# The next batch's z evacuated whole and spread by DMA, VectorE empties one score bank in ten, some VectorE work moved, and the fixed order starts at step ten

## The chip, the cores and the metric

The kernel runs on one core of one Trainium2 chip. The metric is the device time of one execution in microseconds. Before the change the median of three runs is 2632.43 us.

## The reference, cut to what matters

An attention without softmax over 8 batches is followed by a mixture of experts over its rows:

```
scores = (z @ z.T) / S                 # per batch: z is 2496 x 64, S = 2496
out    = relu(scores) ** 2 @ v         # v is 2496 x 256
x      = (u * out).reshape(19968, 256)
logits = x @ w_gate                    # 8 experts
# the (token, expert) pairs in falling order of logit; a token goes to the first expert with room (2496 each)
y[tokens of e] = relu(x[tokens of e] @ w1[e]) @ w2[e]
```

Everything is float32. The kernel splits each operand of a matmul in two parts, hi and lo, and adds three products (hi by hi, lo by hi, hi by lo).

## The kernel before

**Steps.** The attention is a chain of 800 steps, n = 100 b + 20 g + kt: b is the batch, g one of five groups of 512 queries (the last has 448), kt one of 20 tiles of 128 keys (the last has 64 rows). In step n TensorE (PE) adds a key tile to the two accumulators of its group, six matmuls (L893 to L896). What they read, `hi` and `lo`, is made four steps earlier from `r`: ScalarE (ACT) squares `r` in place (L864), ACT (L869) or VectorE (DVE, L871) rounds it to `hi`, DVE subtracts to get `lo` (L880). In this text "step 46" and the like are counted within a batch.

**Tens.** `r` comes from scores made ten at a time. At each step whose number ends in 0 PE writes the scores of steps n+4 to n+13, in five pairs (three matmul pairs each, L851), into PSUM banks named `sc`, of which there are six. Each bank is emptied by one rectification, relu and scale, on ACT (L860). The stretch from the first score matmul of one ten to that of the next is called "ten 0" to "ten 90" below, after its first step; the ten of steps 50 to 59 is ten 50. Whatever else takes an `sc` bank (the transposes of z and of finished outputs) takes it between two tens, in a rotation.

**Around them.** At the end of a group DVE and ACT copy the accumulators out (`at`, L902 and L904), PE transposes them (L916), DVE multiplies by u (L927) and then makes 32 partial dot products with the gate's weights (`lt`, L944, "logits"), one per expert and 128 tokens. A `settle` (L73 to L91) finds the best expert of each of a batch's tokens; it stands at step 46 of the next batch.

**The z of the next batch** is prepared during a batch, for five groups g: loaded with SP's queue (`zin`, L773 and L776, 128 rows by 4 tiles), transposed on PE into an `sc` bank (`z_turn`, L807, at steps 41, 45, 49, 53 and 57), and a step later emptied by `z_parts`: per half of the partitions an ACT copy to `zh` (L818) and a DVE subtraction to `zl` (L819). The score matmuls use two halves of 64 partitions at a time, so every tile must stand in both halves. After the last group `swap_z` copies the missing halves by four DMAs (L824, L825).

**Order.** On PE, ACT and DVE the instructions stand in the order in which the code writes them (`manual_schedule`), from step -4 on. The SP queue is filled by a scheduler. A lookup `todo` tells what stands at which step.

Of the kernel before, what the change touches and what calls it, by code (L numbers as in the profile page):

```python
# [705 lines left out]
def attention(tc, u, v, z, w_gate, xd, identf, made, first, scale):  # L706
# [16 lines left out]
    with ExitStack() as ctx:  # L723
# [44 lines left out]
            return src[b, :NT * 128].rearrange("(p i) d -> p i d", i=NT)  # L768

        def load(src, b, g, name, width, copies):  # L770
            t = io.tile([128, 4, width], F32, name=name)
            n = min(4, NT - 4 * g)
            nc.sync.dma_start(t[:, :n], rows(src, b)[:, 4 * g:4 * g + n])  # L773
            if n < 4:
                for c in range(copies):
                    nc.sync.dma_start(t[c * TL:(c + 1) * TL, n], src[b, NT * 128:])  # L776
            return t
# [16 lines left out]
        def z_turn(b, g):  # L794
            if g == 0:
                ZH[b] = zp.tile([128, KT * 128], F32R, name="zh")
                ZL[b] = zp.tile([128, KT * 128], F32R, name="zl")
            p = ps.tile([128, 512], F32, name="sc", bufs=SCB)
            c = slice(512 * g, 512 * g + 512)
            t = ZI.pop((b, g))  # L800
            if (b, g) == (0, 0):
                for i in range(4):
                    nc.tensor.transpose(p[:, i * 128:i * 128 + 128], t[:, i].rearrange("p s d -> p (s d)"), identf)
                return (nc.scalar.activation(ZH[b][:, c], p, AF.Copy),
                        nc.vector.tensor_sub(ZL[b][:, c], p, ZH[b][:, c].bitcast(F32)))
            for i in range(2):
                nc.tensor.transpose(p[:, i * 128:i * 128 + 128],  # L807
                                    t[:, 2 * i:2 * i + 2].rearrange("p s d -> p (s d)"), identf)
            ZT[b, g] = p

        def z_parts(b, g):
            c = slice(512 * g, 512 * g + 512)
# [28 lines left out]
        def scores(lo, hi):  # L841
            for n in range(lo, hi, 2):
# [9 lines left out]
                                         start=key is ZH and query is ZH, stop=key is ZL)  # L852
                for s in range(2):
                    SC[n + s] = pair[s]
                    rectify(n + s)

        def rectify(n):
            p = SC.pop(n)
            r = wk.tile([128, 512], F32, name="r", bufs=GO + 3)[:, :p.shape[1]]
            recent["r"] = nc.scalar.activation(r, p, AF.Relu, scale=scale)  # L860
            R[n] = r

        def square(n):
# [1 line left out]

        def split_hi(n):
            h = wk.tile([128, 512], F32R, name="hi", bufs=LA + 1)[:, :width(seq[n][1])]
            if n % 5 < 3:
                nc.scalar.activation(h, R[n], AF.Copy)  # L869
            else:  # L870
                nc.vector.tensor_copy(h, R[n])  # L871
            HI[n] = h
# [110 lines left out]

        def logits_at(m0):
            if m0 + KT < B * NQ * KT:
                return [m0 + GO] * 14 + [m0 + KT] * 14 + [m0 + KT + 4 + i for i in range(4)]
            return [m0 + GO] * 16 + [m0 + GO + 1 + i // 3 for i in range(16)]

        for c in range(0, (B - 1) * NT // 16 * 16, 16):
            at((B * NQ - 1) * KT + 2 + c // 16, premask, c, c + 16)  # L990
        for b in range(B - 1):
            at(((b + 1) * NQ + 2) * KT + 6, settle, b * NT, (b + 1) * NT)
        at(B * NQ * KT, settle, (B - 1) * NT, (B - 1) * NT + 4 * (NQ - 1))
        at(B * NQ * KT, premask, (B - 1) * NT // 16 * 16, JP - 16)
        for b in range(B):
# [17 lines left out]
                at(B * NQ * KT + 3, settle, B * NT, J)  # L1013
            if b:
                for g in range(NQ):
                    m = n0 - 3 * KT + 4 * g + 1
                    at(m - 5, load_z, b, g)
                    at(m, z_turn, b, g)
                    at(m + 1, z_parts, b, g)
                    at(n0 - KT + 4 * g - 8, load_v, b, g)  # L1020
                at(n0 - 3 * KT + 4 * NQ + 2, swap_z, b, slice(0, KT * 128))
                for kt in range(KT):
                    at(n0 - KT + kt, split_v, b, kt)
            else:
# [27 lines left out]
        for n in range(-LA, N + 4 * E):  # L1052
            if n == 2:
                early.close()
            if n == -LA:
                fixed.enter_context(tc.manual_schedule(
                    engines={mybir.EngineType.PE, mybir.EngineType.Activation, mybir.EngineType.DVE}))
            if n == N - 4:
# [42 lines left out]
```

## Time and profile before

| what | value |
|---|---|
| median of three runs (lowest, highest) | 2632.43 us (2632.39, 2635.14) |
| the profiled execution | 2634.49 us |
| its span in the trace | 2632.2 us |
| last attention matmul starts | 1505.7 us |
| PE, DVE, ACT, POOL busy | 97%, 77%, 59%, 14% of the span |

The profiled execution lies 2.06 us above the median, and its span 2.3 us below its own time. Engine shares are averages over the attention and the experts' part, which begins when the attention ends. PE is almost always busy, so time can only come from gaps on PE, from matmuls that stand still within their "busy" time, or from matmuls at a lower clock.

### The profile page before, as it was taken

The page shows a single profiled execution, that of the slowest core. Times are in us where ns is not written, and L with a number is a line of the kernel's source. Part 1 is how long each engine was busy: PE and PEld are TensorE (multiplying, and loading weights), DVE is VectorE, ACT ScalarE, POOL GpSimd, SP SyncE. Part 2 cuts the span into 40 slices and gives each one's busy share as a digit, 9 for nine tenths or more (in the row PEclk, how much of TensorE's full clock was granted, in tenths as well). Part 3 has the DMA queues.
Part 4 walks back from the last instruction along what each step waited for, and adds up shares of the span by engine and source line. Part 5 has one row for each costly group of instructions (what it writes and reads, how often), then busy time and mean ns, then how long its engine had stood idle before and what let it go on. Part 6 is the DMA issues. An engine that isn't in the chain of part 4 may idle for free.

```text
span 2632.2 us, 44683 instructions
## 1 busy us (share of the span) xinstructions
PE 2550.8 (97%) x16328; PEld 2142.8 (81%) x16328; DVE 2027.4 (77%) x6142; ACT 1545.2 (59%) x2934; POOL 366.5 (14%) x507
## 2 busy tenths in 40 slices
PE   7999999999999999999999989999999999999998
PEld 5778787787787787787877768888898989889997
DVE  5788788898898898898888878878686868686322
ACT  7788788787788787887888512333333333333332
POOL 2000000000000000000000002242333333334331
PEclk9999999999999999999999989999999999999999
DMA  4121121210220121121200011112121212121110
GB/s 138 41 71 56 40 67 44 58 62 32 63 72 26 53 72 39 41 72 37 68 32 19 22 41 40 55 56 65 44 69 45 70 44 68 45 85 59 45 43 24
DMA packets 71644, 139.61 MB, mean 53 GB/s; under 512 B 12160, under 2 KB 39680, under 8 KB 71424
## 3 DMA queue, kind: packets, MB, share of 16 engines
q1 hardware_dynamic: 56320, 95.84, 11.6%
q0 software_dynamic: 15104, 40.91, 4.9%
q8 instruction: 128, 2.10, 0.3%
q14 instruction: 92, 0.75, 0.1%
HBM read 85.60 MB, written 40.89 MB: 48 GB/s over the span
## 4 chain that ended last, share of the span: by engine, by line
PE 76%; DVE 13%; ACT 6%; issue 3%; DMA 1%; POOL 0%; POOLq 0%; DVEq 0%; ACTq 0%; SPq 0%
PE acc L893 11%; PE acc L896 11%; PE acc L895 10%; PE sc L851 10%; PE y L602 5%; PE hp L571 5%; PE y L604 5%; PE y L603 5%; PE hp L572 5%; PE hp L573 5%; ACT r L864 2%; DVE lt L944 2%; PE srch L243 2%; DVE lo L880 2%; PE xp L555 1%
## 5 line engine op out<-in xcount | busy, mean ns | idle before, releaser
L893 PE MATMUL acc<-hi,vh 128*128 128x512 f32 (+1 forms) x1600 | 633.1, 396 | 1.7 <-DVE hi L877 1.3
L880 DVE TENSOR_TENSOR lo<-r,hi 128x512 fp32r<-128x512 f32 (+1 forms) x760 | 513.0, 678 | 149.7 <-ACT hi L869 137.2
L896 PE MATMUL acc<-hi,vl 128*128 128x512 f32 (+1 forms) x1600 | 617.9, 386 | 0.0
L895 PE MATMUL acc<-lo,vh 128*128 128x512 f32 (+1 forms) x1520 | 588.2, 387 | 0.5 <-DVE lo L880 0.2
L590 ACT ACTIVATE hh<-hp 128x512 fp32r<-128x512 f32 (+1 forms) x320 | 187.8, 587 | 548.2 <-PE hp L573 478.4
L864 ACT ACTIVATE r<-r 128x512 f32<-128x512 f32 (+1 forms) x800 | 477.0, 625 | 0.8
L944 DVE SCALAR_TENSOR_TENSOR lt<-xs,wgb 128x256 bf16<-128x256 f32 x1248 | 448.8, 421 | 0.7
L860 ACT ACTIVATE r<-sc 128x512 f32<-128x512 f32 (+1 forms) x800 | 393.0, 624 | 92.7 <-PE sc L851 91.8
L893 PEld LDWEIGHTS acc<-hi,vh 128*128 128x128 f32 x1600 | 301.5, 189 | 84.8 <-issue 30.1
L602 PE MATMUL y<-w2h,hh 128*128 128x256 f32 (+1 forms) x1280 | 366.2, 286 | 1.4 <-ACT y L629 1.4
L603 PE MATMUL y<-w2l,hh 128*128 128x256 f32 (+1 forms) x1280 | 362.4, 283 | 0.0
L869 ACT ACTIVATE hi<-r 128x512 fp32r<-128x512 f32 (+1 forms) x480 | 298.5, 622 | 106.4 <-issue 54.8
L896 PEld LDWEIGHTS acc<-hi,vl 128*128 128x128 f32 x1600 | 301.3, 188 | 56.8
L895 PEld LDWEIGHTS acc<-lo,vh 128*128 128x128 f32 x1520 | 286.9, 189 | 52.7 <-DVE lo L880 4.0
L571 PE MATMUL hp<-xh,w1h 128*128 128x512 f32 (+2 forms) x646 | 262.3, 407 | 0.7 <-ACT xh L564 0.7
L851 PE MATMUL sc<-zh 64*128 64x512 f32 (+1 forms) x800 | 224.2, 438 | 34.7 <-ACT r L860 18.5
L572 PE MATMUL hp<-xl,w1h 128*128 128x512 f32 (+2 forms) x646 | 250.7, 389 | 0.0
L602 PEld LDWEIGHTS y<-w2h,hh 128*128 128x128 f32 (+1 forms) x1280 | 240.6, 188 | 12.0 <-ACT y L629 1.8
L573 PE MATMUL hp<-xh,w1l 128*128 128x512 f32 (+2 forms) x646 | 249.5, 387 | 0.0
L603 PEld LDWEIGHTS y<-w2l,hh 128*128 128x128 f32 (+1 forms) x1280 | 240.6, 188 | 8.9
L635 POOL DMA_INDIRECT out_dram<-y,idx x160 | 184.5, 1153 | 386.7 <-ACT y L629 338.8
L496 POOL DMA_INDIRECT xg<-xd,idx x160 | 162.8, 1018 | 378.5 <-PE xp L555 133.0
(1156 smaller groups left out, 3805.7 us busy)
## 6 DMA issues: line engine op xcount, KB each, us to landing
vr<-in_v_dram SPq DMA_DIRECT2D x32, 512.0 KB, 3.7
ur<-in_u_dram SPq DMA_DIRECT2D x32, 512.0 KB, 4.3
xd<-xs SPq DMA_DIRECT2D x32, 512.0 KB, 2.9
wr<-in_moe_w_dram SPq DMA_DIRECT2D x32, 512.0 KB, 5.6
zh<-zh SPq DMA_DIRECT2D x14, 320.0 KB, 3.7
zl<-zl SPq DMA_DIRECT2D x14, 320.0 KB, 5.4
zin<-in_z_dram SPq DMA_DIRECT2D x31, 128.0 KB, 2.0
vr<-in_v_dram SPq DMA_DIRECT2D x8, 384.0 KB, 3.3
```

What stands on the lines that cost most here:

```text
L571: nc.tensor.matmul(p[:, c], wh, xh, start=(d == 0), stop=False)
L572: nc.tensor.matmul(p[:, c], wh, xl, start=False, stop=False)
L602: nc.tensor.matmul(o, h[:, c], wh, start=first, stop=False, skip_group_check=True)
L603: nc.tensor.matmul(o, h[:, c], wl, start=False, stop=False, skip_group_check=True)
L851: nc.tensor.matmul(pair[s], key[b][r, k:k + 128], query[b][r, q], start=key is ZH and query is ZH, stop=key is ZL)
L860: recent["r"] = nc.scalar.activation(r, p, AF.Relu, scale=scale)
L864: nc.scalar.activation(R[n], R[n], AF.Square)
L880: recent["l"] = nc.vector.tensor_sub(l, a, h.bitcast(F32))
L893: nc.tensor.matmul(o, vh, h, start=(kt == 0), stop=False)
L895: nc.tensor.matmul(o, vh, l, start=False, stop=False)
L896: nc.tensor.matmul(o, vl, h, start=False, stop=last)
L944: nc.vector.scalar_tensor_tensor(t[r], XS[b, g][r, i], 1.0, WG["rows"][r, e], op0=OP.mult, op1=OP.mult, accum_out=lg[r, j, e:e + 1])
```

## The change

Five edits. (1) `z_parts` and `swap_z` of batches 1 to 7 give way to `z_whole`: ACT and DVE empty the bank at full height into staging tiles `zsh` and `zsl`, of which there is one each, and eight DMAs of 64 KB per group spread them into both halves of `zh` and `zl`. The transposes stand at steps 41, 45, 51, 54 and 57, the load buffers of `zin` are two and not three. (2) In every full ten the second tile's bank is emptied by DVE (L873 after) and not by ACT; in exchange ACT rounds seven `hi` of ten and not six. (3) The logits of the third group of a batch are made 18 in the first ten and 14 in the next (before 14, 14 and 4 over the steps after), those of the fourth group 10, 14 and 8. (4) `settle` stands at step 32 and not 46. (5) The fixed order begins at step 10: before that a scheduler orders PE, ACT and DVE.

```diff
-            t = io.tile([128, 4, width], F32, name=name)
+            t = io.tile([128, 4, width], F32, name=name, bufs=2 if width == DQ else 3)
...
+        def z_whole(b, g):
+            p = ZT.pop((b, g))[:, :256]
+            h, l = [io.tile([128, 256], F32R, name=name, bufs=1) for name in ("zsh", "zsl")]
+            nc.scalar.activation(h, p, AF.Copy)
+            nc.vector.tensor_sub(l, p, h.bitcast(F32))
+            for t, src in ((ZH, h), (ZL, l)):
+                v4 = t[b][:, 512 * g:512 * g + 512].bitcast(F32).rearrange("p (i s q) -> p i s q", s=2, q=128)
+                v3 = src.bitcast(F32).rearrange("p (i q) -> p i q", q=128)
+                for s in range(2):
+                    for half in range(2):
+                        nc.sync.dma_start(v4[DQ * half:DQ * half + DQ, :, s], v3[DQ * s:DQ * s + DQ])
...
-                    rectify(n + s)
+                    rectify(n + s, n + s == lo + 1 and hi - lo == GO)
...
-            recent["r"] = nc.scalar.activation(r, p, AF.Relu, scale=scale)
+            if aside:
+                nc.vector.tensor_scalar(r, p, 0.0, scale, op0=OP.max, op1=OP.mult)
+            else:
+                recent["r"] = nc.scalar.activation(r, p, AF.Relu, scale=scale)
...
-            if n % 5 < 3:
+            if (n - LA) % GO not in (0, 4, 8):
                 nc.scalar.activation(h, R[n], AF.Copy)
...
-                return [m0 + GO] * 14 + [m0 + KT] * 14 + [m0 + KT + 4 + i for i in range(4)]
+                mid, end = {NQ - 3: (18, 14), NQ - 2: (10, 14)}.get(m0 // KT % NQ - 1, (14, 14))
+                return [m0 + GO] * mid + [m0 + KT] * end + [m0 + KT + 4 + i for i in range(4 * E - mid - end)]
...
-            at(((b + 1) * NQ + 2) * KT + 6, settle, b * NT, (b + 1) * NT)
+            at(((b + 1) * NQ + 1) * KT + 12, settle, b * NT, (b + 1) * NT)
...
-                    m = n0 - 3 * KT + 4 * g + 1
+                    m = n0 - 3 * KT + (4 * g + 1 if 4 * g + 2 < GO else KT - 3 * (NQ - g))
                     at(m - 5, load_z, b, g)
                     at(m, z_turn, b, g)
-                    at(m + 1, z_parts, b, g)
+                    at(m + 1, z_whole, b, g)
...
-                at(n0 - 3 * KT + 4 * NQ + 2, swap_z, b, slice(0, KT * 128))
...
-            if n == -LA:
+            if n == GO:
                 fixed.enter_context(tc.manual_schedule(
```

The first place is VectorE at steps 46 to 50 of a batch, before: the end of `settle`, the two halves of a `zl` behind it, and the logits of the next ten.

```order
L78 TENSOR_TENSOR code<-eq 128x19
L79 TENSOR_TENSOR oh<-code,code8b 128x152
L85 TENSOR_SCALAR sign<-m 128x19
L86 SCALAR_TENSOR_TENSOR key<-m,sign 128x19
L106 COPY rep<-key 128x152
L90 TENSOR_SCALAR top<-key 128x19
L91 CAST low<-key 128x19
L819 TENSOR_TENSOR zl<-sc,zh 64x2x128 x2
L944 SCALAR_TENSOR_TENSOR lt,lg<-xs,wgb 128x256
L880 TENSOR_TENSOR lo<-r,hi 128x512 x2
L871 CAST hi<-r 128x512
L880 TENSOR_TENSOR lo<-r,hi 128x512
```

After the change the same engine has no `settle` there. These are its rows from the last but one z of a batch (g = 3, the first `zsl` shown) to the start of ten 60; an `lo` stands between the last `zsl` and the copy of the accumulator, and then comes the rectification.

```order
L886 CAST hi<-r 128x512
L895 TENSOR_TENSOR lo<-r,hi 128x512
L892 TENSOR_TENSOR hi<-r,hi 64x512
L815 TENSOR_TENSOR zsl<-sc,zsh 128x256
L895 TENSOR_TENSOR lo<-r,hi 128x512 x2
L886 CAST hi<-r 128x512
L895 TENSOR_TENSOR lo<-r,hi 128x512
L815 TENSOR_TENSOR zsl<-sc,zsh 128x256
L895 TENSOR_TENSOR lo<-r,hi 128x512
L917 COPY at_6192<-acc_5778 128x512
L873 TENSOR_SCALAR r<-sc 128x512
L959 SCALAR_TENSOR_TENSOR lt,lg<-xs,wgb 128x256 x14
```

What moved: the score bank of each ten's second tile now waits for VectorE, and at the start of ten 60 VectorE comes to it only behind the last two `zsl`.

The second place is SP's queue over the z of a batch. Before, all loads stand ahead of the four copies:

```order
L773 DMA zin<-in_z_dram 128x256
L931 DMA xd<-xs 128x1024
L773 DMA zin<-in_z_dram 128x192
L776 DMA zin<-in_z_dram 64x64 x2
L773 DMA ur<-in_u_dram 128x768
L776 DMA ur<-in_u_dram 64x256 x2
L773 DMA zin<-in_z_dram 128x256 x3
L825 DMA zh<-zh 64x10x128
L824 DMA zh<-zh 64x10x128
L824 DMA zl<-zl 64x10x128
L825 DMA zl<-zl 64x10x128
```

After, from the second group's spread on (the last group, g = 4, is loaded in three pieces: 128x192 and twice 64x64):

```order
L821 DMA zl<-zsl 64x2x128 x4
L773 DMA zin<-in_z_dram 128x256
L776 DMA ur<-in_u_dram 64x256 x2
L773 DMA zin<-in_z_dram 128x192
L776 DMA zin<-in_z_dram 64x64
L821 DMA zh<-zsh 64x2x128 x4
L821 DMA zl<-zsl 64x2x128 x4
L776 DMA zin<-in_z_dram 64x64
L821 DMA zh<-zsh 64x2x128 x4
L821 DMA zl<-zsl 64x2x128 x4
L773 DMA zin<-in_z_dram 128x256
L821 DMA zh<-zsh 64x2x128 x4
```

What moved: forty small copies stand among the loads, and the last piece of the fifth group's load stands behind the eight copies of the third group.

The third place is PE's start. Before, behind the first transposes, come the second four score tiles in pairs and then the first accumulations:

```order
L807 MATMUL sc<-identf,zin 128x128 x2
L851 MATMUL sc<-zh 128x512 x2
L851 MATMUL sc<-zl,zh 128x512 x2
L851 MATMUL sc<-zh,zl 128x512 x2
L851 MATMUL sc<-zh 128x512 x2
L851 MATMUL sc<-zl,zh 128x512 x2
L851 MATMUL sc<-zh,zl 128x512 x2
L893 MATMUL acc_234<-hi,vh 128x512
```

After, three steps of accumulation stand there first, and the scores that follow are partly single:

```order
L807 MATMUL sc<-identf,zin 128x128 x2
L908 MATMUL acc_232<-hi,vh 128x512
L908 MATMUL acc_233<-hi,vh 128x512
...
L863 MATMUL sc<-zh 128x512
L863 MATMUL sc<-zl,zh 128x512
L911 MATMUL acc_232<-hi,vl 128x512
L911 MATMUL acc_233<-hi,vl 128x512
L908 MATMUL acc_232<-hi,vh 128x512
L910 MATMUL acc_232<-lo,vh 128x512
L863 MATMUL sc<-zh,zl 128x512
L863 MATMUL sc<-zh 128x512
```

What moved: scores now stand between accumulations, some of them without the partner that used the other 64 rows.

## Rows read from the trace of the kernel before

**Rows 1.** The page's first part: engine, busy us, share, instructions.

```profile
PE 2550.8 (97%) x16328; PEld 2142.8 (81%) x16328; DVE 2027.4 (77%) x6142; ACT 1545.2 (59%) x2934; POOL 366.5 (14%) x507
```

**Rows 2.** Windows: stretch, us, busy (count) by engine, PEclk, DMA, GB/s; batch 3.

```profile
617.20:635.94 18.74, 18.74 (x99) 15.00 (x98) 16.71 (x55) 14.24 (x27) 0.00 (x0) 1.00 0.17 56
635.94:653.33 17.39, 17.39 (x89) 13.77 (x89) 12.84 (x42) 14.33 (x27) 0.00 (x0) 1.00 0.01 1
653.33:672.80 19.47, 19.47 (x106) 15.65 (x105) 16.58 (x58) 12.56 (x25) 0.00 (x0) 1.00 0.23 67
672.80:695.94 23.14, 20.12 (x94) 15.07 (x94) 17.47 (x56) 18.59 (x36) 0.00 (x0) 0.93 0.07 19
...
750.66:766.58 15.92, 15.92 (x89) 13.73 (x88) 15.75 (x55) 14.81 (x33) 0.00 (x0) 1.00 0.30 76
```

**Rows 3.** PE's timeline at ten 30 and before ten 70: start, us, instruction.

```profile
638.13 0.44 PE L851 MATMUL sc<-zh 64*128 64x512 f32 x2
...
638.82 0.74 PE L851 MATMUL sc<-zh 64*128 64x512 f32 x2
...
639.96 0.50 PE L893 MATMUL acc<-hi,vh 128*128 128x512 f32 x1
...
716.02 0.39 PE L896 MATMUL acc<-hi,vl 128*128 128x512 f32 x1
716.34 0.50 PE L851 MATMUL sc<-zh 64*128 64x512 f32 x2
```

**Rows 4.** Timelines of ACT and of DVE at the start of ten 20.

```profile
618.20 5.01 ACT L860 ACTIVATE r<-sc 128x512 f32<-128x512 f32 x10 [0.75 <-PE sc L851]
...
624.25 0.63 ACT L869 ACTIVATE hi<-r 128x512 fp32r<-128x512 f32 x1
...
625.44 0.63 ACT L869 ACTIVATE hi<-r 128x512 fp32r<-128x512 f32 x1
...
617.54 0.68 DVE L902 COPY at<-acc 128x512 f32<-128x512 f32 x1
```

**Rows 5.** Timelines of PE, ACT and DVE around the start of ten 50.

```profile
677.94 0.49 PE L851 MATMUL sc<-zh 64*128 64x512 f32 x1 [2.62 <-ACT r L860]
...
673.87 0.38 ACT L818 ACTIVATE zh<-sc 64x256 fp32r<-64x256 f32 x1 [5.78 <-DVE zl L819]
...
670.73 0.31 DVE L73 TENSOR_REDUCE m<-lg 128x19 f32<-128x152 f32 x1
...
673.43 0.41 DVE L819 TENSOR_TENSOR zl<-sc,zh 64x256 fp32r<-64x256 f32 x1
```

**Rows 6.** Windows, sums: ten 50, ten 60 (batches 1-6), both in batch 0, ten 0 (seven).

```profile
sum 139.58, PE 121.70 PEld 91.70 DVE 106.12 ACT 111.67 POOL 0.00; mean PE 20.28 PEld 15.28 DVE 17.69 ACT 18.61 POOL 0.00
...
sum 121.75, PE 118.69 PEld 90.33 DVE 111.79 ACT 94.72 POOL 0.00; mean PE 19.78 PEld 15.06 DVE 18.63 ACT 15.79 POOL 0.00
...
sum 40.85, PE 38.61 PEld 29.18 DVE 34.47 ACT 32.66 POOL 0.00; mean PE 19.31 PEld 14.59 DVE 17.23 ACT 16.33 POOL 0.00
...
sum 136.74, PE 136.12 PEld 104.71 DVE 131.83 ACT 110.42 POOL 0.00; mean PE 19.45 PEld 14.96 DVE 18.83 ACT 15.77 POOL 0.00
```

**Rows 7.** SP's timeline, copies between halves: issue time, us.

```profile
44.95 0.59 SPq L824 DMA_DIRECT2D zh<-zh  x1
45.63 0.59 SPq L824 DMA_DIRECT2D zl<-zl  x1
...
698.86 1.07 SPq L825 DMA_DIRECT2D zl<-zl  x1
```

**Rows 8.** DMA issues (tensors, count, KB, median to landing); `zl`'s landings, first 60 us.

```profile
zh<-zh SPq DMA_DIRECT2D x8, 64.0 KB, 2.1
...
zin<-in_z_dram SPq DMA_DIRECT2D x16, 16.0 KB, 2.4
...
DMA to landing us min/median/max: 2.0/2.2/4.9
```

**Rows 9.** Waits of ACT in the first 50 us: in total, times, longest.

```profile
ACT r L860 <- PE sc L851: 5.5, 6, 2.0
```

More of the change, by code (lines that the diff above doesn't have):

```diff
@@ L854, in scores, with rectify @@
                     SC[n + s] = pair[s]
-                    rectify(n + s)
-        def rectify(n):
+                    rectify(n + s, n + s == lo + 1 and hi - lo == GO)
+        def rectify(n, aside):
             p = SC.pop(n)
             r = wk.tile([128, 512], F32, name="r", bufs=GO + 3)[:, :p.shape[1]]
-            recent["r"] = nc.scalar.activation(r, p, AF.Relu, scale=scale)
+            if aside:
+                nc.vector.tensor_scalar(r, p, 0.0, scale, op0=OP.max, op1=OP.mult)
+            else:
+                recent["r"] = nc.scalar.activation(r, p, AF.Relu, scale=scale)
             R[n] = r
```

## The prediction

> **What bounds the kernel now.** I read the page's engine shares first. PE is busy 97% of the span [rows 1], so a gain has to come out of the 3% or out of matmuls that stand still while they count as busy. The change touches the attention alone, and there one ten is like another, so the windows by tens come next. A plain ten is one without z work: ten 20 lasts 18.74 us, ten 30 lasts 17.39 [rows 2] (in ten 20 PE also transposes an output). The tens with z are longer: over batches 1 to 6 ten 50 lasts 139.58/6 = 23.26 us, ten 60 121.75/6 = 20.29 [rows 6], and ten 40 19.47 [rows 2]. Against plain ones (17.39 and 18.74) that is 5.9 + 1.55 + 0.7 us a batch.
>
> Where ten 50 loses it is seen in the three timelines at its start: `settle` takes DVE from 670.73 to 673.43; the `zl` behind it starts at 673.43; ACT's second `zh` copy waits 5.78 us for that `zl` and starts at 673.87; the rectifications queued behind it come late, and PE waits 2.62 us for a score bank until 677.94 [rows 5]. The granted clock of that ten is 0.93 [rows 2]: after this wait some matmuls ran at the lower of the two levels (1.2 against 2.4 GHz), which with the 2.62 and 2 x 0.24 for two transposes makes up the 5.9, so that it costs some 2.7.
>
> A second loss is in every ten, inside busy time. Pairs 4 and 5 of the scores start at 638.13 and 638.82, 0.69 us apart: three matmuls at 0.23. Pair 5 takes until 639.96, 1.14 us. A change from accumulation to scores costs about 0.09 (716.02 to 716.34 is 0.32 and not 0.23); I take the same for the way back. So pair 5 stands 1.14 - 0.69 - 0.09 = 0.36 us [rows 3]. It needs banks 3 and 4 of the six again, and ACT empties ten banks in 5.01 us [rows 4], one per 0.50, while PE fills one per 0.35.
>
> **The change, part by part.**
>
> *A bank on DVE.* ACT then empties nine, and every bank behind the second comes free 0.50 us earlier, more than the 0.36 that pair 5 stands. DVE must have emptied its bank when pair 4 or 5 asks for it, about 2.1 us into the ten. In a ten that begins with the copy of an accumulator, that copy runs 617.54 to 618.22, 1.02 us into ten 20 [rows 2, 4]; the new rectification reads the same shape from PSUM, so I price it at the copy's 0.68: it ends at 1.7 and has some 0.4 to spare. Gain 0.36 per plain ten. Such tens are 10, 20, 30, 70, 80 and 90 of batches 0 to 6 and eight of batch 7: 42 + 8 = 50, so **18.0 us**. Bounds: 0 (DVE too late everywhere) and 25 (0.50 a ten). The `hi` that goes from DVE to ACT cancels in sum; ACT has 3 us free in a ten.
>
> *Settle.* 673.43 - 670.73 = 2.70 us of DVE [rows 5] goes to ten 30, where DVE is busy 12.84 of 17.39 us [rows 2]: 15.54, still under. I cost it at nothing there; were the cover gone, each batch would lose up to 2.7 - 1.85 = 0.85.
>
> *Logits.* Eight of 32 leave tens 80 and 90, four of them for ten 70, four from one group's later steps for its first. In ten 90 DVE is busy 15.75 of 15.92 us [rows 2], so the rectification's 0.68 finds its room only because logits leave; sum nothing, with 0.4 either way per batch.
>
> *z, the old costs.* A transpose pair costs PE (19.47 - 18.74)/3 = 0.24 [rows 2]: ten 40 has three. Now two stand in ten 40, three in ten 50, so without waits the tens cost 18.38 + 0.50 = 18.88, 17.03 + 0.75 = 17.78 and 18.38, with 18.38 = 18.74 - 0.36 and 17.03 = 17.39 - 0.36.
>
> *z, the new wait.* With one `zsh` and one `zsl`, a group's copies must have landed before the next group may be staged. Copies of just this size are in the trace: 64 KB between halves are issued 45.63 - 44.95 = 0.68 us apart [rows 7] and land 2.1 us after issue [rows 8]. So four last 3 x 0.68 + 2.1 = 4.1 us, eight 6.9. The clock runs from the first score matmul of ten 50, a step is 6 x 0.23 = 1.38:
> - ACT rectifies nine banks from 1.0 (618.20 - 617.20) [rows 2, 4] to 5.5, does two and a half squares with `hi` (1.19 each, 625.44 - 624.25 [rows 4]) and reaches `zsh` of g = 2 at 8.2; it takes 0.38 (673.87's row [rows 5]). Copies issued at 8.6, the fourth lands at 12.7. `zsl`'s copies are issued from 11.3 and land by 15.4.
> - SP issues the last piece of g = 4's load behind these eight, at 14.0. It lands 2.4 later [rows 8], at 16.4. PE reaches that group's transpose at 15.25 and **waits 1.15**.
> - `zsh` of g = 3 can only be written at 12.75, `zsl` at 15.45, and its copies land at 18.7 and 21.4. So `zsl` of g = 4 starts on DVE at 21.45. Behind it on DVE stand an `lo`, the accumulator's copy and then ten 60's rectification [the order above], 0.41 + 3 x 0.68 in all: it ends at 23.75. Ten 60 starts at 19.3 and wants that bank at 21.7: **PE waits 2.05**, together with the stop of about 1 us before it for g = 4's own bank, in two pieces. Waits of 1 us are shorter than the 2.62 before, so I expect no loss of clock.
>
> So tens 40, 50, 60 become 18.88, 17.78 + 1.15 = 18.93, 18.38 + 2.05 = 20.43: 58.24 us against 19.47 + 23.26 + 20.29 = 63.02. Gain 4.78 in six batches, **28.7**; in batch 0 they are 19.46 + 40.85 = 60.31 [rows 6], gain **2.1**.
>
> The Trainium skill's page "DMA: Bandwidth & Descriptors", section "Rules for kernel authors", says to coalesce many small transfers into one large one, because at under 64 KB one pays mostly overhead; this change goes the other way, from 4 to 40 copies a batch. The rows above show the overhead as a latency that overlaps: eight copies in 6.9 us and not in 8 x 2.1 = 16.8. Were they one behind another, each group's eight would last 9.9 longer; two groups in the chain make 19.8, and with the clock's 2.7 that is some 22 us a batch in place of the 3.2 here.
>
> *Ten 0.* It lasts 136.74/7 = 19.53 [rows 6], 0.79 over ten 20, because ACT comes late from the next batch's v. With nine banks it catches up in part; I take 0.4 of a possible 1.15 (0.79 + 0.36): 7 x 0.4 = **2.8**, bounds 0 and 8.
>
> *The start.* A free order can fill waits: ACT waits 5.5 us there for scores [rows 9]. But score matmuls without their partner do half the work in 0.23 us, and a dozen stand alone. I take **2.0**, between +6.6 and -3.
>
> *The experts' part* keeps its instructions: nothing.
>
> **The sum.** 18.0 + 28.7 + 2.1 + 2.8 + 2.0 = 53.6. The profiled execution took 2634.49, so it would take 2580.9; it lies 2.06 above the median, 2632.43, which becomes **2579 us**. The terms' bounds give 2568 to 2592 where this mechanism holds.
>
> **The rivals.** A measurement of this kernel tells 0.2%, 5.3 us, from no change.
> - *The z waits vanish*: the copies land early enough or other engines take the slack. For it: the landing row's minimum is 2.0, and DVE and ACT have free time. Against: one buffer each, and 13.8 us of copies for two groups in 18. 3.2 us x 7 less: 2557.
> - *The bank comes late on DVE.* For it: DVE is 77% busy on average [rows 1] and 15.75 of 15.92 us in ten 90; it has only 0.4 us to spare behind the copy. If it comes as late as ACT did, the 18.0 and half of the 0.36 in z tens go, and with them part of the start: about 27 less, 2606.
> - *The copies land late.* The longest landing of a small copy is 4.9 [rows 8], not 2.1. In ten 60, where v is loaded too, each group in the chain then takes 2.8 more, 5.6 for the two groups ahead of it, of which I let 4.2 a batch reach PE: + 29, 2608.
> - *Slower than before*: SP issues at its longest pitch, 1.07 [rows 7], and copies land at 4.9. Then four copies last 8.1 us and eight 12.4, g = 4's transpose waits about 4.4 and ten 60 about 7.5, and such waits would bring the lower clock of ten 50 back (2.7): 14.6 a batch for 3.2, + 80: 2659. It decides from 3.2 + 53.6/7 = 10.8 us of z waits a batch; at that point nothing is gained.
> - *Copies one behind another* (the cost per copy that the page's rule makes of it, + 19 x 7): about 2710.
>
> **How the numbers follow.** My sum 55%; z waits vanish 12%; bank late 17%; copies late 8%; slower 5%; no gain within 5.3 us 3%, some mixture of bank and copies both late. Of the five for slower, one is the copies one behind another. The range leaves out the slower end and the far side of the fastest: 2556 to 2612. Faster 0.90, same 0.04, slower 0.06.
>
> **What the profile after would show.** Ten 30 at 17.0 and ten 20 at 18.4, with pair 5 at 0.8 us and not 1.14. Ten 50 at about 19 and a clock of 1.00 in all of it, with no wait of ACT for `zl`. A wait of PE for the load of g = 4 of about 1.15, and of about 2 in ten 60 for a bank that DVE or the z evacuation holds. ACT waiting for DMAs before `zsh` of g = 3 and 4, DVE before `zsl`. SP's issues 0.68 apart, landing in 2.1. It would be wrong if the DVE bank's rectification started later than 1.5 us into the ten, if a wait over 2 us stood in tens 50 or 60 with a clock below 1.00, or if tens 80 and 90 grew longer, DVE being full there.

## The result and the profile after

The changed kernel takes 2609.21 us (median of five runs, 2603.54 to 2616.02), the kernel before 2635.09 (five runs). The ratio is 0.9905, with an interval of 0.9887 to 0.9924: faster by 25 us. The forecast was 2579, a gain of 53.6. The direction was right, and the gain a little under half of the forecast one. The profiled execution took 2609.21, its span is 2607.4, 24.8 less than before.

The page of the changed kernel: PE's busy time, and the small copies (count, KB, median us to landing).

```profile
PE 2522.9 (97%) x16328; PEld 2137.9 (82%) x16328; DVE 2016.1 (77%) x6105; ACT 1543.1 (59%) x2901; POOL 358.7 (14%) x507
...
zh<-zsh SPq DMA_DIRECT2D x140, 64.0 KB, 2.1
zl<-zsl SPq DMA_DIRECT2D x140, 64.0 KB, 2.0
```

Half of the copies land within 2.0 to 2.1 us of their issue, as forecast; a few take longer, which comes back below. Next the windows of the changed kernel (stretch, us, busy time and count of PE, PEld, DVE, ACT, POOL, granted clock, DMA share, GB/s): tens 20, 30, 40, 50 and 60 of batch 5, and ten 60 of batch 3. They answer to [rows 2].

```profile
976.51:994.97 18.46, 18.46 (x100) 14.95 (x100) 16.70 (x54) 14.61 (x27) 0.00 (x0) 1.00 0.17 58
...
994.97:1012.11 17.14, 17.14 (x90) 13.76 (x90) 15.15 (x55) 14.36 (x27) 0.00 (x0) 1.00 0.01 1
...
1012.11:1031.04 18.93, 18.93 (x103) 15.24 (x103) 16.53 (x55) 15.15 (x29) 0.00 (x0) 1.00 0.28 82
...
1031.04:1049.85 18.81, 18.09 (x96) 14.22 (x96) 14.18 (x45) 13.74 (x26) 0.00 (x0) 1.00 0.35 93
1049.85:1071.25 21.40, 19.17 (x101) 14.79 (x100) 17.14 (x55) 16.26 (x30) 0.00 (x0) 1.00 0.34 99
...
685.65:709.43 23.78, 20.71 (x100) 15.74 (x100) 17.38 (x55) 16.37 (x30) 0.00 (x0) 0.93 0.31 89
```

Tens 20 to 50 stand where the forecast put them: 18.46 (18.38), 17.14 (17.03), 18.93 (18.88), 18.81 (18.93). The long stall of ten 50 (23.26 before) is gone, and its clock is 1.00. Ten 60 is the place that failed: 21.40 in place of 20.43, and in batch 3 23.78, with part of it at the lower clock. The sums over the places of [rows 6] follow: ten 50 of batches 1 to 6, ten 60 of batches 0 to 6 (22.26 of it batch 0's), ten 0 seven times.

```profile
sum 114.75, PE 108.69 PEld 85.29 DVE 81.23 ACT 82.41 POOL 0.00; mean PE 18.11 PEld 14.22 DVE 13.54 ACT 13.74 POOL 0.00
...
sum 154.82, PE 137.24 PEld 105.56 DVE 120.52 ACT 114.02 POOL 0.00; mean PE 19.61 PEld 15.08 DVE 17.22 ACT 16.29 POOL 0.00
...
sum 139.15, PE 134.02 PEld 104.96 DVE 136.02 ACT 115.68 POOL 0.00; mean PE 19.15 PEld 14.99 DVE 19.43 ACT 16.53 POOL 0.00
```

With the starts of all tens the 24.8 us can be laid out by place (rounded):

| place | forecast gain, us | measured gain, us |
|---|---|---|
| 48 plain tens (without tens 10 and 20 of batch 0) | 17.3 | 14.5 |
| tens 40 to 60, batches 1 to 6 | 28.7 | 17.2 |
| tens 40 to 60, batch 0 | 2.1 | 0.1 |
| ten 0, seven times | 2.8 | -2.4 |
| the start up to ten 30 of batch 0, with its two plain tens | 2.7 | -4.2 |
| behind the last scores | 0 | -0.3 |

**Ten 60** is read from the timelines of the changed kernel, batch 5: PE, then DVE, ACT and SP.

```profile
1051.34 0.39 PE L863 MATMUL sc<-zh 64*128 64x512 f32 x1
1053.13 0.50 PE L863 MATMUL sc<-zh 64*128 64x512 f32 x1 [1.40 <-DVE zsl L815]
...
1053.71 0.39 PE L863 MATMUL sc<-zh 64*128 64x512 f32 x1
1054.93 0.50 PE L863 MATMUL sc<-zh 64*128 64x512 f32 x1 [0.83 <-DVE r L873]
...
1052.66 0.42 DVE L815 TENSOR_TENSOR zsl<-sc,zsh 128x256 fp32r<-128x256 f32 x1 [3.12 <-DMA zl<-zsl]
...
1054.20 0.68 DVE L873 TENSOR_SCALAR r<-sc 128x512 f32<-128x512 f32 x1
...
1044.05 0.39 ACT L814 ACTIVATE zsh<-sc 128x256 fp32r<-128x256 f32 x1 [1.20 <-DMA zh<-zsh]
...
1045.92 2.54 SPq L821 DMA_DIRECT2D zh<-zsh  x4
1048.56 2.54 SPq L821 DMA_DIRECT2D zl<-zsl  x4
```

Read from the bottom: four copies take SP 2.54 us. The eight of g = 3 have left SP by 1051.10; when they have landed, DVE may write the one `zsl` again, at 1052.66, after 3.12 us of standing. PE stops 1.40 us for the bank that this frees, goes on for 1.0 us, and stops again for the bank of the rectification at 1054.20, which stands behind the `zsl`. The waits of the changed kernel from 140 us on, so from ten 60 of batch 0 (engine and line, waited for: us in total, times, longest):

```profile
DVE zsl L815 <- DMA zl<-zsl: 37.2, 12, 4.2
...
ACT zsh L814 <- DMA zh<-zsh: 21.1, 10, 3.9
...
PE sc L863 <- DVE zsl L815: 11.8, 7, 2.3
...
PE sc L807 <- DMA zin<-in_z_dram: 6.1, 6, 1.8
PE sc L863 <- DVE r L873: 5.8, 7, 0.8
```

Both stops come in each of the seven batches that prepare a z. The first is 1.31 to 2.25 us long, the second 0.83 or 0.84. What makes the first longer is seen in batches 0, 1 and 3: the first stop, the window of ten 60, and for batch 3 SP's issue of the last four copies of g = 3 and how long the copies took to land from g = 3 on; the last line is the same for g = 3 of batch 5.

```profile
143.20 0.50 PE L863 MATMUL sc<-zh 64*128 64x512 f32 x1 [2.25 <-DVE zsl L815]
...
139.06:161.32 22.26, 19.17 (x99) 14.82 (x99) 17.14 (x55) 16.25 (x30) 0.00 (x0) 1.00 0.32 95
...
325.07 0.49 PE L863 MATMUL sc<-zh 64*128 64x512 f32 x1 [1.73 <-DVE zsl L815]
...
321.46:344.72 23.26, 20.69 (x99) 15.81 (x99) 17.39 (x55) 16.37 (x30) 0.00 (x0) 0.93 0.31 91
...
689.77 0.50 PE L863 MATMUL sc<-zh 64*128 64x512 f32 x1 [2.23 <-DVE zsl L815]
...
684.20 3.54 SPq L821 DMA_DIRECT2D zl<-zsl  x4
...
DMA to landing us min/median/max: 2.0/2.0/3.7
...
DMA to landing us min/median/max: 2.0/2.0/2.1
```

In batch 3 some copies land 3.7 us after issue, SP needs 3.54 us for the next four and not 2.54, and `zsl` starts 1.0 us later than in batch 5. Batch 0 has the same longest landing of 3.7, batch 1 one of 3.2. In batches 2, 4 and 5 no copy of g = 2 and 3 takes over 2.1, and the first stop is 1.40 to 1.42. (In batch 6 the longest is 3.0, but ten 60 itself begins 1 us later there, and the stop is 1.31.) The lower clock follows in batches 1 and 3, and not in batch 0, whose first stop is the longest of all.

**The start and ten 0.** The first two windows are those of the kernel before, from the scores of step 8 to ten 20 and ten 20 of batch 0; the next two are the same of the changed kernel, with a granted clock of 0.81 and 19.86 us. Behind them stand the last of PE's stops in that first stretch, and its stop in ten 20.

```profile
37.10:61.07 23.97, 22.17 (x108) 16.69 (x109) 13.74 (x29) 20.66 (x43) 0.00 (x0) 1.00 0.33 92
61.07:79.83 18.76, 18.76 (x99) 14.99 (x99) 13.42 (x22) 14.24 (x27) 0.00 (x0) 1.00 0.18 65
...
37.88:64.19 26.31, 24.33 (x96) 17.11 (x96) 15.65 (x31) 20.91 (x43) 0.00 (x0) 0.81 0.30 85
64.19:84.05 19.86, 18.91 (x99) 14.89 (x98) 12.60 (x20) 14.72 (x27) 0.00 (x0) 1.00 0.15 53
...
45.58 0.79 PE L863 MATMUL sc<-zh 64*128 64x512 f32 x1 [0.86 <-ACT zh L830]
...
67.72 0.50 PE L863 MATMUL sc<-zh 64*128 64x512 f32 x1 [0.94 <-DVE r L873]
```

The timelines of ScalarE and VectorE show where the first rectification of each stands in a ten 0 that begins at 939.50.

```profile
942.01 4.49 ACT L875 ACTIVATE r<-sc 128x512 f32<-128x512 f32 x9
...
942.90 0.68 DVE L873 TENSOR_SCALAR r<-sc 128x512 f32<-128x512 f32 x1
```

Here ACT starts 2.51 us into the ten (2.29 to 2.66 over the seven), where it started at 1.74 to 1.89 before, and DVE at 3.40.

### The profile page after: what moved, and what is told of

Read it like the earlier page. It is cut to its first block, busy times and chain, and to the rows that moved or that the text cites. A ratio compares the mean times of both kernels' runs of the same rounds, so it can differ in the third digit from the quotient of the medians.

```text
span 2607.4 us, 44969 instructions
## 1 busy us (share of the span) xinstructions
PE 2522.9 (97%) x16328; PEld 2137.9 (82%) x16328; DVE 2016.1 (77%) x6105; ACT 1543.1 (59%) x2901; POOL 358.7 (14%) x507
## 4 chain that ended last, share of the span: by engine, by line
PE 82%; DVE 10%; ACT 3%; DMA 2%; issue 1%; SPq 1%; POOL 0%; POOLq 0%; DVEq 0%; ACTq 0%
PE acc L908 13%; PE acc L911 12%; PE acc L910 12%; PE sc L863 10%; PE y L602 5%; PE hp L571 5%; PE y L604 5%; PE y L603 5%; PE hp L572 5%; PE hp L573 5%; PE srch L243 2%; PE sc L931 1%; PE xp L555 1%; ACT r L879 1%; DMA zl<-zsl 1%
## 5 line engine op out<-in xcount | busy, mean ns | idle before, releaser
L895 DVE TENSOR_TENSOR lo<-r,hi 128x512 fp32r<-128x512 f32 (+1 forms) x760 | 504.2, 677 | 115.2 <-ACT hi L884 105.6
L884 ACT ACTIVATE hi<-r 128x512 fp32r<-128x512 f32 (+1 forms) x560 | 348.3, 622 | 140.2 <-issue 83.9
L875 ACT ACTIVATE r<-sc 128x512 f32<-128x512 f32 (+1 forms) x722 | 364.2, 611 | 90.7 <-PE sc L863 84.8
L635 POOL DMA_INDIRECT out_dram<-y,idx x160 | 176.7, 1105 | 385.3 <-ACT y L629 337.5
L863 PE MATMUL sc<-zh 64*128 64x512 f32 (+1 forms) x800 | 192.7, 424 | 26.6 <-DVE zsl L815 11.8
```

Of the source, the lines that this page charges most:

```text
L863: nc.tensor.matmul(pair[s], key[b][r, k:k + 128], query[b][r, q], start=key is ZH and query is ZH, stop=key is ZL)
L895: recent["l"] = nc.vector.tensor_sub(l, a, h.bitcast(F32))
```

## The experiments

Each kernel ran with the kernel before on the same chip. Four of them (all banks of ten 60 on ScalarE, the two with the last v moved, the logits where they were) ran on a chip where the kernel before takes 2682.65 us; for those the text gives ratios, gains over the kernel before, and the windows of tens.

### The start with the fixed order

```diff
-            if n == GO:
+            if n == -LA:
                 fixed.enter_context(tc.manual_schedule(
```

> The changed kernel with the fixed order from step -4 again, as before the change; nothing else differs. Theory A (the free start lets single score matmuls and transposes stand between accumulations and late z copies stop PE again and again, after which the first full ten of scores runs at the lower clock): ten 20 of batch 0 starts at about 60.5 us (64.2 in the changed kernel, 61.1 before) and lasts 18.5 and not 19.86; the kernel is 4 to 5.5 us faster than the changed one, about 2604. Theory B (the start is bound by the loads of the first batch, whatever the order): ten 20 starts at 63 to 65 again and the time stays within 1 us.

Measured: 2611.21 us, ratio 0.9909 (0.9893 to 0.9926), the same as the changed kernel. Ten 20 of batch 0 started 2.7 us earlier, at 61.53, much as theory A said, but lasted 22.21, so that nothing was gained. Both theories fall. The timelines of this kernel in ten 20 (DVE, then PE) show what was missing:

```profile
61.70 2.31 DVE L748 COPY wgb<-wg 128x1024 f32<-128x1024 f32 x2
...
65.14 0.67 DVE L873 TENSOR_SCALAR r<-sc 128x512 f32<-128x512 f32 x1
...
65.86 0.50 PE L863 MATMUL sc<-zh 64*128 64x512 f32 x1 [1.74 <-DVE r L873]
```

VectorE makes the gate's weights, 2.31 us, just ahead of the first score bank that it now empties at a group's end. PE waits 1.74 us for it, and the pairs behind run at the lower clock: their matmuls follow each other at 0.43 us and not 0.23.

### Two staging tiles

```diff
-            h, l = [io.tile([128, 256], F32R, name=name, bufs=1) for name in ("zsh", "zsl")]
+            st = io.tile([128, 512], F32R, name="zs", tag="ztwo", bufs=2)
+            h, l = st[:, :256], st[:, 256:]
```

(The tile of batch 0's first z lends its place, with two buffers too.)

> The changed kernel with two staging tiles for z (both halves in one tile, two of them) in place of one zsh and one zsl; order and copies are the same. Theory A (one staging tile chains each group to the landing of the eight copies of the group before, and the last zsl on VectorE holds back the rectification in ten 60): VectorE's and ScalarE's waits for these copies go, ten 60 of batches 0 to 6 falls from 21.3 to 23.8 to 18.8 to 19.2 us, the kernel is 17 to 24 us faster than the changed one, 2585 to 2592, and its runs spread less. Theory B (SP's queue is the limit: 24 copies at 0.65 us stand one behind another, with the last load piece of the fifth group among them): PE's wait for that load stays and the fifth group comes late anyway; ten 60 falls by under 1 us, the time by under 7.

Measured: 2579.44 us, ratio 0.9788 (0.9771 to 0.9804), 30 us below the changed kernel, more than theory A said. The windows of ten 60, batches 0 to 6, sum to 129.27 where the changed kernel has 154.82:

```profile
sum 129.27, PE 129.27 PEld 104.53 DVE 116.81 ACT 102.19 POOL 0.00; mean PE 18.47 PEld 14.93 DVE 16.69 ACT 14.60 POOL 0.00
```

Of the waits, this one is left:

```profile
PE sc L807 <- DMA zin<-in_z_dram: 5.7, 6, 1.2
```

A mean of 18.47 is a plain ten: both stops are gone. What remains is PE's wait for the last piece of the fifth group's load, in ten 50: SP's queue costs that 1 us a batch, so theory B falls. In this kernel too the slowest of the small copies took 4.7 us to land. With a second staging tile that reaches PE nowhere in ten 60; with one, it does.

### All banks of ten 60 on ScalarE

```diff
-                    rectify(n + s, n + s == lo + 1 and hi - lo == GO)
+                    rectify(n + s, n + s == lo + 1 and hi - lo == GO and lo % (NQ * KT) != 60 + LA)
```

> The changed kernel with one staging tile each, but in ten 60 of each batch ScalarE empties all ten banks. Theory A (ten 60 holds two stops in turn, first for the bank that z of the fifth group still occupies, about 1.5 us, then for VectorE's bank, whose rectification stands behind the last zsl, about 1 us): the second goes, the first stays; ten 60 falls to 20.2 to 20.6 in all batches and does not fall to the lower clock, the time by 8 to 13 us to 2596 to 2601. Theory B (the second stop is only the first one's shadow, the bank of z would hold pair 5 as long): ten 60 stays above 21 and the time within 4 us of 2609.

Measured: ratio 0.9859 (0.9842 to 0.9875). The gain over the kernel before is 37.8 us where the changed kernel had 25.9, 12 more. The windows of ten 60, batches 0 to 6:

```profile
sum 144.93, PE 134.06 PEld 105.22 DVE 115.54 ACT 116.15 POOL 0.00; mean PE 19.15 PEld 15.03 DVE 16.51 ACT 16.59 POOL 0.00
```

Five lie at 20.0 to 20.4, two at 21.1 and 22.35, the last with a clock of 0.92. Theory A for five batches: the second stop goes, the first stays. Its "all batches" and "does not fall to the lower clock" fail in the other two.

### Before, with the bank on VectorE, settle and logits, but z as it was

The edits (2), (3) and (4) of the change, made in the kernel before.

> The kernel before with three of the five edits: the bank on VectorE with the new split of hi, settle at step 32, the moved logits. z goes as before, by halves and four copies, and the order is fixed from step -4. Theory A (ten 50's long wait was settle ahead of a zl and nothing else): ten 50 falls to 17.8 to 18.2 without z_whole, ten 60 to 19.5 to 20, and the kernel takes 2580 to 2590, less than the changed one. Theory B (the halved evacuation of z itself, each ScalarE half waiting for a VectorE half, holds the rectifications): ten 50 stays above 19.5 and ten 60 above 20, and the kernel takes 2605 to 2618, as long as the changed one or longer.

Measured: 2619.77 us, ratio 0.9937 (0.9921 to 0.9954). The windows of tens 50 and 60, batches 1 to 6:

```profile
sum 113.74, PE 111.03 PEld 83.42 DVE 87.81 ACT 89.44 POOL 0.00; mean PE 18.50 PEld 13.90 DVE 14.63 ACT 14.91 POOL 0.00
...
sum 144.80, PE 129.19 PEld 97.70 DVE 118.06 ACT 106.40 POOL 0.00; mean PE 21.53 PEld 16.28 DVE 19.68 ACT 17.73 POOL 0.00
```

Ten 50 falls to 18.96 without any change to z. That is theory A's cause, though not its 17.8 to 18.2. But ten 60 goes from 20.29 to 24.13, and the time is near theory B's. PE's two stops in ten 60 of batch 3 say what it stands for:

```profile
697.49 0.47 PE L851 MATMUL sc<-zh 64*128 64x512 f32 x1 [1.83 <-DVE zl L819]
699.36 1.28 PE L851 MATMUL sc<-zh 64*128 64x512 f32 x2 [0.56 <-ACT r L863]
```

It waits for the bank that the second `zl` of g = 4 frees, and then for the rectifications on ScalarE; for VectorE's it does not wait. So the evacuation by halves itself stops PE in ten 60 once ten 50 no longer stops it first. The kernel before shows the same in batch 0, which has a z and no `settle` (tens 50 and 60):

```profile
116.67:135.94 19.27, 18.71 (x93) 14.13 (x92) 14.95 (x47) 15.72 (x32) 0.00 (x0) 1.00 0.09 24
135.94:157.52 21.58, 19.91 (x99) 15.05 (x98) 19.51 (x60) 16.93 (x32) 0.00 (x0) 1.00 0.39 110
```

Its ten 50 has no long stall, and its ten 60 is 1.3 us longer than in batches 1 to 6. What the moved bank and logits add to the rest of the 24.13 was not tried by itself.

### Settle back at step 46, with two staging tiles

```diff
-            at(((b + 1) * NQ + 1) * KT + 12, settle, b * NT, (b + 1) * NT)
+            at(((b + 1) * NQ + 2) * KT + 6, settle, b * NT, (b + 1) * NT)
```

> Two staging tiles, settle back at step 46. Theory A (what stalled ten 50 was ScalarE's second half copy waiting for a VectorE subtraction behind settle; the whole evacuation has no such second copy, so ScalarE goes on): ten 50 rises by under 1 us, only by what VectorE's own bank comes late; time under 2586. Theory B (any VectorE work of 2.7 us there holds up ten 50, now through the bank on VectorE): ten 50 rises to 21 to 23.5, partly at the lower clock, and the time to 2593 to 2606.

Measured: 2581.42 us, ratio 0.9792 (0.9776 to 0.9808). Ten 50 of batches 1 to 6:

```profile
sum 114.28, PE 111.28 PEld 84.93 DVE 94.27 ACT 91.85 POOL 0.00; mean PE 18.55 PEld 14.16 DVE 15.71 ACT 15.31 POOL 0.00
```

The same as with settle moved (114.33 with two staging tiles alone). Theory A: the stall of [rows 5] needed both, `settle` at that place and a second ScalarE copy that waited behind it. Here the stall is gone with `settle` in its old place, in the experiment before with z in its old form (with the bank and logits moved as well), and in the kernel before ten 50 takes 19.27 in batch 0, with no `settle`, and 17.39 in batch 7, with no z.

### No bank on VectorE, with two staging tiles

```diff
-                    rectify(n + s, n + s == lo + 1 and hi - lo == GO)
+                    rectify(n + s, False)
...
-            if (n - LA) % GO not in (0, 4, 8):
+            if n % 5 < 3:
```

> Two staging tiles, but ScalarE empties all ten banks and hi is split as before the change. Theory A (the bank on VectorE is worth what the plain tens show): plain tens go back to 17.39, 18.75, 17.30, 17.00 and 15.9, that is 0.3 each for 49 plain tens and 0.3 for each z ten, ten 0 falls to 19.5 or 19.6; in sum 15 to 20 us slower than two staging tiles alone, 2594 to 2600. Theory B (it costs as much as it gives, since VectorE is late at several places): within 5 us of 2579.4.

Measured: 2596.43 us, ratio 0.9854 (0.9838 to 0.9871), 17 above two staging tiles alone. Tens 10, 20, 30 and 70 go back to 17.39, 18.74, 17.39 and 17.29, each 0.3 longer, ten 0 falls to 19.74. Theory A.

### Ten 0: ScalarE or VectorE?

Two edits, one in the changed kernel (all banks of ten 0 on ScalarE), one with two staging tiles (VectorE rounds the tenth tile and not the ninth):

```diff
+                    rectify(n + s, n + s == lo + 1 and hi - lo == GO and lo % (NQ * KT) != LA)
...
+            if (n - LA) % GO not in (0, 4, 9):
```

> The changed kernel, but in ten 0 of each batch all ten banks are emptied by ScalarE. Theory A (ten 0 grew from 19.53 to 19.88 because VectorE comes to its bank only 3.4 us into the ten, behind the accumulator copy and a vl): ten 0 falls to 19.5 or below, the time by about 2.5 to 5 us. Theory B (it grew because ScalarE rounds the tile that stands just ahead, and so starts its rectifications 0.74 us later, at 2.5 and not 1.77 us): with a tenth bank on the same late ScalarE ten 0 rises to 20.2 or so, the time by about 2 us.

> Two staging tiles, and of the three hi that VectorE rounds in ten, the tenth tile's takes the place of the ninth's; so ScalarE no longer rounds the tile just ahead of the next ten's rectifications. Theory A (ten 0 is 20.0 because ScalarE begins there 2.5 us into the ten): ScalarE begins 0.6 us earlier, ten 0 falls to 19.3 to 19.6 and the kernel by 2.5 to 4.5 us, to about 2576. Theory B (VectorE's rectification at 3.4 us into the ten is the limit by itself): ten 0 stays at 19.8 to 20.1, the time within 1 us of two staging tiles alone, 2579.4.

The first took 2613.47 us (0.9922, 0.9906 to 0.9939), ten 0 rose to a mean of 20.37: theory B, ScalarE is late. The second took 2585.21 (0.9808, 0.9791 to 0.9824), ten 0 stayed at 19.88 to 20.25 and ten 90 grew from 15.47 to 15.83: again theory B on ten 0, VectorE is the limit; the time, 5.8 us above and not within 1, neither theory had. In it ScalarE starts at 1.99 to 2.36, but VectorE's rectification at 3.44 to 3.80. So both stand at the limit, and freeing one leaves the other.

### The gate's copies behind ten 20, and the fixed start

```diff
-        at(18, gate_rows)
+        at(21, gate_rows)
...
-            if n == GO:
+            if n == -LA:
```

> Two staging tiles, the fixed order from step -4 as before the change, and VectorE's two copies of the gate's weights (2.31 us) at step 21 and not 18. Theory A (those copies stand ahead of the rectification of ten 20 in batch 0, which is why that ten took 22.2 us with the fixed order and 18.76 before; the free start itself costs some 2.7 us): ten 20 of batch 0 starts at about 61.5 and lasts 18.45, ten 30 starts at 80.0 and not 82.65 as with two staging tiles alone; the time falls by 2.5 to 3, to about 2577. Theory B (the gate's copies do not matter, ten 20 waits for something else there): ten 20 of batch 0 stays over 21 and the time over 2579.

Measured: 2578.84 us, ratio 0.9783 (0.9766 to 0.9799). Ten 20 of batch 0 starts at 61.43 and lasts 18.47; ten 30 starts at 79.90 and not 82.65. Theory A in the trace. The time is only 0.6 us below that of two staging tiles, less than the runs of either spread (3 us).

### The last v behind ten 0, alone and with the tenth hi

In the kernel of the last experiment:

```diff
-                    at(n0 - KT + kt, split_v, b, kt)
+                    at(n0 + kt - (KT if kt < 16 else 5), split_v, b, kt)
```

> The kernel of two staging tiles, fixed start and gate copies at step 21, and the split of the last four key tiles of v (kt 16 to 19) of each next batch at steps 11 to 14 of that batch, in place of 96 to 99 of the one before. Theory A (in ten 0 both ScalarE, which starts its rectifications 2.63 us into the ten, and VectorE, which comes to its bank at 3.52, are late because of the v casts and subtractions just ahead): both come about 1 us earlier, scores end at 4.3 to 4.6 us and not 5.34, ten 0 falls from 20.09 to 19.0 to 19.4 and the kernel by 5 to 8 us, to about 2572. Theory B (ScalarE and VectorE are late there for the work of the group's end, whatever the v does): ten 0 stays over 19.7 and the time within 3 us of 2578.8.

> As the run with v behind ten 0, and VectorE rounds the tenth tile's hi in place of the ninth's. Theory A (ScalarE starts 0.6 us earlier by it, and VectorE, relieved of the v, no longer limits as it did with this edit alone): ten 0 falls further, to 18.6 to 18.9, 2 to 4 us below the other. Theory B (VectorE is still the limit there): ten 0 no shorter than in the other run, ten 90 longer by 0.2 to 0.5, the time 0 to 4 us above it.

The first: ratio 0.9778 (0.976 to 0.9796). Ten 0 sums over seven batches, in the kernel of the last experiment and then in this one:

```profile
sum 140.67, PE 134.15 PEld 105.08 DVE 137.50 ACT 117.09 POOL 0.00; mean PE 19.16 PEld 15.01 DVE 19.64 ACT 16.73 POOL 0.00
```

```profile
sum 134.89, PE 132.23 PEld 104.19 DVE 129.14 ACT 108.28 POOL 0.00; mean PE 18.89 PEld 14.88 DVE 18.45 ACT 15.47 POOL 0.00
```

20.10 falls to 19.27: theory A, with VectorE's busy time in the ten down from 19.64 to 18.45. The last scores of the attention start at 1427.5 us, 5.6 earlier, as expected; the ratio moved by half a thousandth, which its interval does not tell from nothing. (The two kernels ran on different chips, and the 47 us that the kernel before takes longer on the second hide a gain in the ratio; over the kernel before, each gains 62.6 and 56.7 us, 5.9 apart.) The second edit on top: 0.9798 (0.9781 to 0.9814), ten 0 at 19.41, ten 90 longer by 0.4, the time 7 us above. Theory B, and more than its 0 to 4.

### The logits where they were

In the kernel with the gate's copies moved:

```diff
-                mid, end = {NQ - 3: (18, 14), NQ - 2: (10, 14)}.get(m0 // KT % NQ - 1, (14, 14))
-                return [m0 + GO] * mid + [m0 + KT] * end + [m0 + KT + 4 + i for i in range(4 * E - mid - end)]
+                return [m0 + GO] * 14 + [m0 + KT] * 14 + [m0 + KT + 4 + i for i in range(4)]
```

> The kernel of two staging tiles, fixed start and gate copies at step 21, with the logits where they were before the change (14, 14 and 4 for each group). Theory A (tens 80 and 90 have no room on VectorE for its bank unless logits leave): tens 80 and 90 rise from 16.77 and 15.39 to 17.0 and 15.8 to 16.2, the time by 3 to 8 us. Theory B (the room is there anyway): both tens within 0.1 us, the time within 2 us of 2578.8.

Measured: ratio 0.9816 (0.9799 to 0.9832), a gain of 50.3 us over the kernel before; the same kernel with moved logits, on the other chip, had 0.9783 and 56.7 us. Ten 90, seven times:

```profile
sum 118.06, PE 111.46 PEld 95.87 DVE 113.42 ACT 108.18 POOL 0.00; mean PE 15.92 PEld 13.70 DVE 16.20 ACT 15.45 POOL 0.00
```

16.87 for 15.39, while ten 80 stays at 16.7: theory A for ten 90, where VectorE has no room, theory B for ten 80. Ten 0 falls by 0.7, so that 5.7 us remain by the start of the last scores.

## Why the prediction was half right

**Right: the stall of ten 50, and that it goes.** 23.26 became 19.12 (114.75/6; 18.93 forecast) without loss of clock. That moving `settle` and evacuating z whole each suffice for it was not seen.

**Right in kind, 2.8 us short: the bank on DVE.** A plain ten gained 14.5/48 = 0.30 and not 0.36. Taken out of the kernel with two staging tiles, together with its split of `hi`, it is worth 17 us. The 0.36 took the change from scores to accumulation to cost as much as the change back, 0.09. In a ten 30 of the changed kernel the last two matmuls of pair 5 and the first of the accumulation show it at 0.17:

```profile
998.29 0.47 PE L863 MATMUL sc<-zh,zl 64*128 64x512 f32 x2
998.69 0.50 PE L908 MATMUL acc<-hi,vh 128*128 128x512 f32 x1
```

They start 0.40 apart, where 0.23 is the pace.

**Wrong in size: "PE waits 2.05".** The chain itself was right nearly to the tenth: from the start of ten 50, `zsl` of g = 4 was to start at 21.45 and did at 1052.66 - 1031.04 = 21.62; the rectification was to end at 23.75 and ended at 23.84. (Two of its sums slip: 5.5 and two and a half times 1.19 make 8.5, not 8.2, and 21.45, 0.41 and 3 x 0.68 make 23.90; neither matters much.) What failed is the last line of the working. It set the start of ten 60 at 19.3, where the same sum makes ten 50 18.93 long (18.81 here), and it let PE want the bank 2.4 us into the ten, where the part on the bank on DVE had 2.1. With those two terms of its own the wait is 23.75 - 18.93 - 2.1 = 2.72. Measured, ten 60 is 21.40 - 18.44 = 2.96 over a plain one in the batches whose copies all land in time.

The rest of ten 60 is landings and clock. The working took 2.1 for every copy; in batches 0, 1 and 3 some took 3.2 to 3.7, and their ten 60 is 0.9, 1.9 and 2.4 longer, in batches 1 and 3 with loss of clock, which "I expect no loss of clock" had excluded. All in all 11.5 of the 28.7 and 2.0 of the 2.1 were not had, nearly half of the 28.8 us between the forecast gain and the 24.8 of the trace; the start is 6.9 of them, ten 0 5.2 and the plain tens 2.8. The rival "The z waits vanish" was about the right alternative kernel: with a second staging tile the waits in ten 60 vanish. The rivals at 2606 and 2608 lie near the measured time by chance: "the bank comes late" gave up the plain tens, which came, and "the copies land late" priced at 29 us what cost about 5.

**Wrong: ten 0.** "The `hi` that goes from DVE to ACT cancels in sum" counted the engines' work and not its place. One of the seven `hi` now stands just ahead of the next ten's rectifications. Where ScalarE has slack, that is free; in ten 0, where it is busy with v, it starts 0.75 us later, and VectorE's bank, which the slack of "some 0.4" was worked out for only in plain tens, comes at 3.4 us and not 1.0. The forecast gain of 2.8 became a loss of 2.4. Neither edit is the cause alone: with the `hi` moved ten 0 stayed at 20.1, with all its banks on ScalarE it was 20.37, and with bank and `hi` both as before it fell to 19.74, for the 19.53 of the kernel before. Tens 90 and 0 together took 15.90 + 19.53 = 35.43 before and 15.60 + 19.88 = 35.48 after, so the forecast gain of ten 90 was given back in ten 0 as well. Moving four v splits away from there, shown by the two sums of ten 0, gives 0.83 a batch.

**Wrong: the start.** "A free order can fill waits" was guessed at 2.0 from a wait of ScalarE. What the order does to PE was not asked: single score matmuls and transposes stood between accumulations, PE stopped, and the ten behind ran with a granted clock of 0.81. The free start makes ten 20 of batch 0 begin at 63.0 to 64.9 in the kernels with a bank on VectorE and at 61.3 in the one without, the fixed one at 61.1 to 61.8 in all but the kernel with the tenth `hi`, where it is 62.7. The rest, 19.86 for 18.45 with the free order and 22.21 with the fixed one, is the gate's copies ahead of VectorE's first late bank, a place that the prediction did not look at. With the fixed order their move alone brings ten 20 back to 18.47; with the free order only the stop of 0.94 above points to them.

**The Trainium skill's rule.** The Trainium skill's page "DMA: Bandwidth & Descriptors", section "Rules for kernel authors", says to coalesce many small transfers, because under 64 KB one pays mostly overhead. These copies are of just 64 KB. Four were issued in 2.54 us, 0.64 apart, and half landed within 2.0 to 2.1 us (the slowest in 4.5), overlapping; with two staging tiles they cost ten 60 nothing, and what is left is the 1 us a batch that a load waits behind them in SP's queue. So "one behind another", the rival at 2710, did not happen.

What stays open: why a few of the copies land late, and why the lower clock followed the stops in some batches and not in others.

## What to carry to other kernels

Cutting one transfer into many cost little here once its source had a second buffer (and as long as no urgent load stands behind the pieces in the queue); with one, the landing time, and every late landing, became a chain through every engine that fills it, so count buffers before copies. When work moves between engines, look at what stands directly ahead of the time-critical instruction on its new engine at each special place (first group, last group, boundary), not at the sum. And a sum of waits must use its own earlier terms: the start of a stage is the end of the one before in the new timeline, not in the old one.

## What the runs showed of the hardware

The length of a stop alone did not decide on the clock. In ten 60 PE stood still twice, parted by 1.0 us of matmuls: 2.23 and 0.83 us in batch 3 and 1.73 and 0.84 us in batch 1 were followed by matmuls at the lower of the two levels (0.93 over the ten); 2.25 and 0.83 us in batch 0 and 1.40 and 0.83 us in batch 5 were not (1.00). With the fixed start a single stop of 1.74 us in ten 20 was.

Copies of 64 KB from SBUF to SBUF were issued 0.64 us apart and landed 2.0 us after issue in the median, 4.5 at most, and a late one held up SP's next issues (3.54 us for four in place of 2.54).

The kernel before took 47 us longer on another chip (2682.65 for 2635.56). The plain tens of the kernels that ran there agree with the others to 0.1 us; the time lies in the experts' part. From the start of the last scores to the end, the kernel with v behind ten 0 took 1190.0 us there, the kernel that it was made from 1144.6 on the first chip. Why was not looked into; it means that a change is judged by its gain over the kernel before on the same chip.
